# A third seven-product unit in a two-layer convolution and MLP kernel, with the next unit's rows combined early and transposed late

## The chip, the cores and the metric

The kernel runs on one core of one Trainium2 chip. The metric is the device time of one execution in microseconds. Below, PE is TensorE (PEld its weight loads), DVE is VectorE, ACT is ScalarE, POOL is GpSimd, and SP is the queue that issues nearly all DMAs. A "q" behind an engine's name means its instruction queue. L12 is line 12 of the kernel before.

## The reference

A block A (a gated long convolution) and a block B (an MLP) alternate, twice each, over 2048 tokens of width 1024. Everything is float32.

```python
def _A_ref(q, k, v, shift_k, ssm_k, ssm_D):
    k_shift = ...                       # causal depthwise convolution with 4 taps
    kv = k_shift * v
    y = irfft(rfft(kv, 2S) * rfft(ssm_k, 2S))[:S] + kv * ssm_D
    return q * y
def _B_ref(x, w1, b1, w2, b2):
    h = jnp.einsum("bsd,df->bsf", x, w1) + b1
    r = jnp.where(h > zero, h, zero)
    return jnp.einsum("bsf,fd->bsd", r * r, w2) + b2
x = A_q
x = x + _A_ref(_layernorm(x), A_k, A_v, A_shift_k, A_ssm_k, A_ssm_D)
x = x + _B_ref(_layernorm(x), B_w1, B_b1, B_w2, B_b2)
x = x + _A_ref(_layernorm(x), A_k, A_v, A_shift_k, A_ssm_k, A_ssm_D)
x = x + _B_ref(_layernorm(x), B_w1, B_b1, B_w2, B_b2)
```

The convolution y depends on k, v and the filters only, not on x, so it is computed once and used in both layers. The hidden width F of B is 3584.

## The kernel before, in words

**Units.** The tokens are cut into four blocks of 512 (T). A unit is one layer (an A and a B) for one block: `ORDER` (L35) lists eight, numbered 0 to 7 here; units 5, 6 and 7 are (layer 0, block 3), (layer 1, block 2) and (layer 1, block 3). While TensorE runs the MLP of one unit, the other engines and gaps make the convolution of later blocks (`prod_stream`, L502, `fwd_stream`, L483). Its results go to `YD` in DRAM; `done` holds the finished blocks.

**Matmuls in three.** To keep float32 accuracy, each operand is split into a high and a low part, and each product is three matmuls of 128x128 by 128x512 (`mm3`, L317 to L320). A weight tile is loaded (`w_load`, L891), its high part cast by ScalarE (`w_hi`, L907, L913), the low part subtracted by VectorE (`w_lo`, L916, L921). For some tiles (`split_kept`, L864) the pair is stored after the first use (`w_store`, L925) and later loaded whole (L911, the rows "whl<-wd_m").

**Steps.** A list of steps written out in advance sets the order. In a plain unit a step is 12 matmuls with one weight tile: 56 steps of the first layer (w1, "m1") and 56 of the second (w2, "m2"), 112 in all. The weights run ahead of their step by fixed counts: loaded 8 ahead (`W_LOAD`), paired ones and the high parts 4 ahead, the low parts 3 ahead (L37, `w_advance`, L931). All DMAs go through SP in program order, and every engine works its instructions in program order too. `Later` (L65) puts an action a number of steps later: `lag.at(k, fn)`.

**Units with seven products.** Units in `WINO` (L50) do the second layer by Winograd's form of Strassen's scheme: blocks of two hidden tiles by two token halves by two output halves need seven block products instead of eight. `add_wino` (L801) writes their steps: 56 of the first layer as before, and 98 of the second, of 6 matmuls each (14 pairs of hidden tiles by 7 products, in four groups of 3, 3, 4 and 4 pairs, `WCH`); 154 in all. `relu_w` (L1341) makes the activations' sums and their splits. Four of the seven products use combined weights, which `make_t` (L1321) computes once from w2 and writes to `TD` in DRAM; they are loaded with kind "t" (L900). The results of the products gather in `wacc` (`load_wacc`, L1377; `add_b2w`, L1388; `evict_w`, L1393) and are merged at the end (`merge_w`, L1400, L1403) and stored (`store_w`, L1405, L1408). The products of a group run in the order `WORD`, in the last group `WORD_END` (L54).

**Preparing the next unit.** Where the next unit is another block, `prep_a` (L715) takes the first layernorm's statistics of the next rows in mid-unit, and `prep_b` (L732) does the rest near the end: per row tile of 128 tokens it loads the rows x and the convolution's y (L706, L743), combines them on VectorE (L750, L751), takes the second layernorm's statistics (L677 to L695), stores the combined rows to `X1` (L756), normalizes with two passes of ScalarE per half (L712, L713), transposes on TensorE (L770) and splits into xh (ScalarE, L778) and xl (VectorE, L780). It begins when 18 steps are left, and when 30 are left in a `WINO` unit (`PREP_LEFT`, L1549), where its stages stand one and a half times as far apart. The next unit's first matmuls read xh and xl.

**Shared buffers.** `yt` (two of 128x512) takes y; `px` (two of 128x1024) takes rows and the bias b2; the convolution's tiles in the pool `cv` (cp, cx, cg, yh, yl, fx, fg, fk, fy, sm) are used by `make_t`, `relu_w` and `wacc` once the convolution is over.

Of the kernel before, what the change touches and what calls it, by code (L numbers as in the profile page):

```python
# [10 lines left out]
F32 = mybir.dt.float32  # L11
F32R = mybir.dt.float32r  # L12
# [7 lines left out]
P = 128  # L20
# [29 lines left out]
WINO = (6, 7)  # L50
WMAKE = 5
WCH = (3, 3, 4, 4)
WHALF = T // 2
WORD, WORD_END = (0, 1, 3, 4, 5, 6, 2), (0, 3, 5, 6, 4, 2, 1)  # L54
AHEAD_F = (6, 5)
# [174 lines left out]
def tile_h3_mlp(ctx: ExitStack, tc: tile.TileContext, q, kT, vT, shk, ssmT, ssmD, w1, b1, w2, b2,  # L230
# [501 lines left out]
    def prep_b(l, b, lag, mul=2):  # L732
# [49 lines left out]
        for tt in range(NT):  # L782
            st = {}
            for k, d in enumerate((1, 4, 5, 6, 7, 8, 9)):
                lag.at((3 * tt + d) * mul // 2, stage, st, tt, k)
        return xh, xl

# [76 lines left out]
    def split_kept(key):  # L864
        k, c, a, i = key
        if k == "t":
            return False
# [7 lines left out]
    ring, now = [], [0]  # L875

# [14 lines left out]
    def w_load():  # L891
# [7 lines left out]
        if k == "t":  # L899
            SY.dma_start(raw, TD[c][:, a])  # L900
# [420 lines left out]
    def make_t():  # L1321
        for p in range(FT // 2):
            b = [cv.tile([P, 2, 512], F32, name=nm, bufs=n) for nm, n in (("cp", 3), ("cx", 2))]
            for e in range(2):
                f = 2 * p + e
                SY.dma_start(b[e], w2[f * P:(f + 1) * P].rearrange("f (h d) -> f h d", h=2))
            yield
            yield
            yield
            t = [cv.tile([P, 2, 512], F32, name="cg", bufs=2), cv.tile([P, 2, 512], F32, name=("yh", "yl")[p % 2], bufs=1)]  # L1330
# [6 lines left out]
            for e in range(2):  # L1337
                SY.dma_start(TD[p][:, 2 * e:2 * e + 2], t[e])
# [61 lines left out]
    def merge_w(wacc, *ops):  # L1400
        for d, x in ops:
            for n in range(2):
                V.tensor_add(wacc[d][n], wacc[d][n], wacc[x][n])  # L1403

    def store_w(wacc, b, j):  # L1405
        t0, h = {1: (0, 0), 2: (0, 1), 3: (2, 0), 6: (2, 1)}[j]
        for n in range(2):
            SY.dma_start(tokens(out, b, t0 + n)[:, h * 512:(h + 1) * 512], wacc[j][n])  # L1408
# [139 lines left out]
    tgen = None  # L1548
    PREP_LEFT = {u: 30 for u in WINO}  # L1549
# [13 lines left out]
    for s, (k, u, c, a, i, tts, w) in enumerate(steps):  # L1563
# [3 lines left out]
        if u != cur_u:  # L1567
# [4 lines left out]
            if u in WINO:  # L1572
                wacc, rp = {}, {}
                lag.at(6, load_wacc, wacc, b)
                lag.at(8, load_b2, bst)
                lag.at(12, add_b2w, bst, wacc)
# [6 lines left out]
            if u == WMAKE:  # L1583
                tgen = make_t()
# [28 lines left out]
        elif k == "w2":  # L1613
# [10 lines left out]
            if i == done_at - 1:  # L1624
                end = c == len(WCH) - 1
                lag.at(1, evict_w, os, wacc, a, c)
                if end:
                    if a == 5:
                        lag.at(1, merge_w, wacc, (5, 0))
                    elif a == 6:  # L1630
                        lag.at(1, merge_w, wacc, (6, 5))
# [132 lines left out]
```

## Time and profile before

| | |
|---|---|
| median of 3 runs | 2822.39 us (2821.4 to 2832.8) |
| profiled execution | 2829.91 us, its span 2828.1 us |
| TensorE busy | 2724.4 us, 96% of the span |
| VectorE busy | 1854.0 us, 66% |
| ScalarE busy | 1043.1 us, 37% |
| GpSimd busy | 921.3 us, 33% |
| moved by DMA | 759.99 MB, mean 269 GB/s |

How to read the profile: it is of one execution, with times in us from the start of its span. Busy time counts instructions at work, not queues that wait. The 40 slices are 70.7 us each, in tenths of the slice. PEclk is the clock that TensorE was granted, in tenths of full speed. "idle before <-releaser" names what ended an engine's idle time. Matmuls are pipelined: the duration of one overlaps the next, so the distance between starts tells the pace.

### The profile page before, as it was taken

The numbers are of one execution on the slowest core, as the hardware profiler recorded it, in microseconds if no ns is written. First come the engines' busy times: TensorE is split into PE (matmuls) and PEld (weight loads), VectorE is DVE, ScalarE is ACT, GpSimd is POOL, SyncE is SP. The second block draws the span as 40 slices with busy tenths as digits, with TensorE's granted clock in tenths as the row PEclk, the third lists the DMA queues.
The fourth block names the chain that finished last, engine by engine and source line by source line (L and its number), as shares of the span: only waits on it lengthen the run. The fifth ranks groups of instructions, "written<-read, shape, count | busy, mean of one in ns | idle before, by whom it ended". The sixth has DMA issues, their size and how long they took to land.

```text
span 2828.1 us, 36014 instructions
## 1 busy us (share of the span) xinstructions
PE 2724.4 (96%) x12616; PEld 2261.1 (80%) x12616; DVE 1854.0 (66%) x2827; ACT 1043.1 (37%) x1797; POOL 921.3 (33%) x651
## 2 busy tenths in 40 slices
PE   7899899799999999999999999999999999979998
PEld 6787787688888788888888888888888888758887
DVE  8868789777777777779767754264335555564456
ACT  3254344342334333342234322242224434434333
POOL 6826656155552645326552553001000100001000
PEclk9899999899999999999999999999999999989999
DMA  8489999779988798888978786478976675666565
GB/s 253 161 285 354 361 326 318 270 251 340 301 278 304 272 339 291 279 305 298 353 241 280 288 305 214 164 268 314 344 274 231 227 270 172 205 224 216 201 210 163
DMA packets 348166, 759.99 MB, mean 269 GB/s; under 512 B 41928, under 2 KB 130128, under 8 KB 347984
## 3 DMA queue, kind: packets, MB, share of 16 engines
q1 hardware_dynamic: 347984, 757.68, 78.1%
q8 instruction: 100, 1.64, 0.2%
q14 instruction: 82, 0.67, 0.1%
HBM read 611.80 MB, written 145.75 MB: 268 GB/s over the span
## 4 chain that ended last, share of the span: by engine, by line
PE 76%; DVE 8%; DMA 7%; issue 2%; POOL 2%; ACT 2%; SPq 1%; DVEq 0%; POOLq 0%; ACTq 0%
PE p L319 24%; PE p L320 24%; PE p L318 24%; DMA wd_m<-whl 2%; DMA cg<-gd 1%; DMA wr<-w 1%; DVE whl L921 1%; PE pt L319 1%; PE pt L320 1%; PE pt L318 1%; DMA whl<-wd_m 1%; DVE sm L512 1%; DMA cx<-xd 1%; PE p L770 1%; DVE st L677 0%
## 5 line engine op out<-in xcount | busy, mean ns | idle before, releaser
L508 POOL TENSOR_TENSOR cp<-cx,cg 128x384 f32<-128x384 f32 (+5 forms) x288 | 539.6, 1887 | 590.9 <-DVE sm L512 358.9
L318 PE MATMUL p<-xh,whl 128*128 128x512 f32 (+1 forms) x1840 | 708.0, 385 | 2.5 <-DMA whl<-wd_m 2.4
L320 PE MATMUL p<-xh,whl 128*128 128x512 f32 (+1 forms) x1840 | 705.3, 383 | 1.6 <-DVE whl L921 1.0
L319 PE MATMUL p<-xl,whl 128*128 128x512 f32 (+1 forms) x1840 | 704.9, 383 | 0.3 <-DVE xl L1234 0.3
L318 PE MATMUL p<-whl,rh 128*128 128x512 f32 x1512 | 606.5, 401 | 7.5 <-DMA whl<-wd_m 5.7
L319 PE MATMUL p<-whl,rh 128*128 128x512 f32 x1512 | 601.4, 398 | 5.4 <-DVE whl L921 5.4
L320 PE MATMUL p<-whl,rl 128*128 128x512 f32 x1512 | 600.3, 397 | 0.0
L913 ACT CAST whl<-wr 128x512 fp32r<-128x512 f32 x506 | 307.0, 618 | 478.7 <-PE p L320 286.3
L921 DVE TENSOR_TENSOR whl<-wr,whl 128x512 fp32r<-128x512 f32 x492 | 394.6, 818 | 101.7 <-ACT whl L913 99.4
L320 PEld LDWEIGHTS p<-xh,whl 128*128 128x128 f32 x1840 | 347.1, 189 | 69.7 <-DVE whl L921 1.4
L318 PEld LDWEIGHTS p<-xh,whl 128*128 128x128 f32 x1840 | 347.3, 189 | 68.9 <-issue 2.8
L319 PEld LDWEIGHTS p<-xl,whl 128*128 128x128 f32 x1840 | 347.2, 189 | 66.1 <-DVE xl L1234 0.5
L1318 DVE TENSOR_TENSOR rl<-wr,rh 128x512 fp32r<-128x512 f32 x168 | 166.9, 994 | 314.8 <-ACT rh L1313 314.6
L318 PEld LDWEIGHTS p<-whl,rh 128*128 128x128 f32 x1512 | 287.5, 190 | 73.8 <-DMA whl<-wd_m 6.8
L319 PEld LDWEIGHTS p<-whl,rh 128*128 128x128 f32 x1512 | 287.5, 190 | 72.0 <-DVE whl L921 7.7
L320 PEld LDWEIGHTS p<-whl,rl 128*128 128x128 f32 x1512 | 287.3, 190 | 67.4
L1310 ACT ACTIVATE wr<-p,b1t 128x512 f32<-128x512 f32 x166 | 114.5, 690 | 505.7 <-PE p L320 501.2
L512 DVE TENSOR_REDUCE sm<-cp 128x128 f32<-128x384 f32 (+5 forms) x288 | 249.7, 875 | 27.4 <-POOL cp L508 27.3
L1391 POOL TENSOR_TENSOR acc<-acc,px 128x512 f32<-128x512 f32 x12 | 16.8, 1434 | 602.6 <-DMA px<-b 602.6
L1413 DVE TENSOR_TENSOR acc<-p,acc 128x512 f32<-128x512 f32 x184 | 122.8, 688 | 125.7 <-PE p L320 125.1
L1355 DVE TENSOR_TENSOR rl<-wr,rh 128x256 fp32r<-128x256 f32 (+1 forms) x56 | 32.1, 574 | 175.5 <-ACT rh L1350 175.5
L1524 POOL TENSOR_TENSOR acc<-acc,px 128x1024 f32<-128x1024 f32 x24 | 65.3, 2750 | 181.4 <-DMA td<-yl 169.8
(240 smaller groups left out, 3124.1 us busy)
## 6 DMA issues: line engine op xcount, KB each, us to landing
whl<-wd_m SPq DMA_DIRECT2D x488, 512.0 KB, 4.9
wr<-w SPq DMA_DIRECT2D x402, 256.0 KB, 5.2
wd_m<-whl SPq DMA_DIRECT2D x70, 512.0 KB, 6.1
wr<-td SPq DMA_DIRECT2D x112, 256.0 KB, 4.2
cx<-xd SPq DMA_DIRECT2D x48, 512.0 KB, 5.2
cg<-gd SPq DMA_DIRECT2D x48, 512.0 KB, 7.3
gd<-fg SPq DMA_DIRECT2D x72, 256.0 KB, 5.5
cx<-xd SPq DMA_DIRECT2D x48, 384.0 KB, 6.1
```

Of the source, the lines that this page charges most:

```text
L318: PE.matmul(o, lh, rh, start=start, stop=False)
L319: PE.matmul(o, lh, rl, start=False, stop=False)
L320: PE.matmul(o, ll, rh, start=False, stop=stop)
L508: G.tensor_mul(pr.rearrange("p c i -> p i c"), xt[:, 0:j + 1], gt[:, j::-1])
L512: V.tensor_reduce(sm[:, ty, jj], st["pr"], axis=AX.X, op=OP.add)
L913: A.copy(t[:, 0], raws[n]["t"])
L921: ENG[e[n % len(e)]].tensor_sub(t[:, 1], raws[n]["t"], t[:, 0].bitcast(F32))
L1310: A.activation(r, st["o"], AF.Relu, bias=b1t[:, st["f"]:st["f"] + 1])
L1318: V.tensor_sub(st["lo"], st["r"]["t"], st["hi"].bitcast(F32))
L1355: V.tensor_sub(st["lo"], r[:, 0:n], st["hi"].bitcast(F32))
L1413: V.tensor_add(accs[tt][:, d], o, accs[tt][:, d])
L1524: G.tensor_add(a, a, st["t"])
```

## The change

`WINO` becomes (5, 6, 7), so unit 5 does its second layer with seven products as well; its result goes to `X2` instead of the output. `make_t` begins one unit earlier: from unit 4 on, as soon as all blocks of the convolution are done, one turn a step (not in the last 18 steps of unit 4), in half-size parts through other buffers (sm, the convolution's tables fh and fl, and yt), and a load of a combined weight that is not made yet runs `make_t` until it is. Eight combined weights (pairs 10 to 13, two of four tiles) are kept split. In units with seven products `prep_w` takes the place of `prep_b`: 84 steps before the end it begins to combine the next rows, take their statistics and store them to `X1`, one row tile every 13 steps; 32 steps before the end it begins to load them again, normalize them in one ScalarE pass per half, transpose and split, one row tile every 6 steps. The flag `ytbusy` keeps `make_t` from beginning a part while yt holds y. The merges of a unit's end come 3 steps later and its stores 6 (in the last unit the stores 3, but for product 1); the loads of `wacc` and b2 and the bias's addition come 5, 4 and 4 steps later.

The diff, cut to its core:

```diff
--- before.py
+++ after.py
@@ -47,11 +47,15 @@
 PACE_SLACK = {1: 74, 3: 10}
 PACE_TO = {1: 2}
 PLAIN = 1
-WINO = (6, 7)
-WMAKE = 5
+WINO = (5, 6, 7)
+WMAKE = 4
+W_PREP, W_XN = 84, 32
+T_KEPT = 10
 WCH = (3, 3, 4, 4)
 WHALF = T // 2
 WORD, WORD_END = (0, 1, 3, 4, 5, 6, 2), (0, 3, 5, 6, 4, 2, 1)
+WEND = {0: (), 3: (), 5: ((1, 1, 5, 0),), 6: ((1, 1, 6, 5), (2, 1, 3, 6), (2, 0, 3), (3, 1, 6, "x"), (3, 1, 1, 0)),
+        4: ((1, 1, 6, 4), (1, 0, 6), (2, 1, 5, 4), (2, 1, 2, 5)), 2: ((1, 0, 2),), 1: ((1, 0, 1),)}
 AHEAD_F = (6, 5)
 KEEP_F = 3
 CHAIN = ((2, 3, 3, 4, 5, 6, 7, 11, 12, 12, 13), (5, 6, 7, 7, 8, 8, 9, 9, 10, 10, 11))
@@ -729,7 +733,7 @@
         lnx[l, b] = mv, rstd_b(ve, sd)
         yield
 
-    def prep_b(l, b, lag, mul=2):
+    def prep_b(l, b, lag):
         mv, r = lnx.pop((l, b))
         xh = mw.tile([P, KT, T], F32R, name="xh", bufs=1)
         xl = mw.tile([P, KT, T], F32R, name="xl", bufs=1)
@@ -782,8 +786,79 @@
         for tt in range(NT):
             st = {}
             for k, d in enumerate((1, 4, 5, 6, 7, 8, 9)):
-                lag.at((3 * tt + d) * mul // 2, stage, st, tt, k)
+                lag.at(3 * tt + d, stage, st, tt, k)
         return xh, xl
+
+    def load_xy(l, b, tt):
+        x, y = load_x(l, b, tt), []
+        for h in range(2):
+            yt = ml.tile([P, 512], F32, name="yt", bufs=2)
+            SY.dma_start(yt, YD[b][:, tt, h * 512:(h + 1) * 512])
+            y.append(yt)
+        return x, y
+
+    def combine(x, y, m, r):
+        for h in range(2):
+            sl = slice(h * 512, (h + 1) * 512)
+            V.scalar_tensor_tensor(y[h], x[:, sl], m, y[h], op0=OP.subtract, op1=OP.mult)
+            V.scalar_tensor_tensor(x[:, sl], y[h], r, x[:, sl], op0=OP.mult, op1=OP.add)
+
+    def prep_w(l, b, lag):
+        mv, r = lnx.pop((l, b))
+        xT = []
+        sts = [{} for _ in range(NT)]
+
+        def early(tt, k):
+            st = sts[tt]
+            if k == 0:
+                st["x"], st["y"] = load_xy(l, b, tt)
+                ytbusy[0] = True
+            elif k == 1:
+                combine(st["x"], st.pop("y"), mv[:, tt, 0:1], r[:, tt:tt + 1])
+                ytbusy[0] = False
+            elif k == 2:
+                st["mv"] = pre.tile([P, 1, 2], F32, name="mv2", bufs=4)
+                stats(st["x"], st["mv"][:, 0])
+                st["ve"], st["sd"] = rstd_a(st["mv"])
+            elif k == 3:
+                SY.dma_start(X1[b][:, tt], st.pop("x"))
+                st["r"] = rstd_b(st["ve"], st["sd"])
+                st["nr"] = pre.tile([P, 1], F32, name="nr", bufs=4)
+                V.scalar_tensor_tensor(st["nr"], st["mv"][:, 0, 0:1], -1.0, st["r"], op0=OP.mult, op1=OP.mult)
+
+        def late(tt, k):
+            st = sts[tt]
+            if k == 0:
+                st["x"] = pre.tile([P, D], F32, name="px", bufs=2)
+                SY.dma_start(st["x"], X1[b][:, tt])
+            elif k == 1:
+                for h in range(2):
+                    sl = slice(h * 512, (h + 1) * 512)
+                    A.activation(st["x"][:, sl], st["x"][:, sl], AF.Identity, bias=st["nr"], scale=st["r"])
+            elif k == 2:
+                if not xT:
+                    xT.extend(mw.tile([P, KT, T], F32R, name=nm, bufs=1) for nm in ("xh", "xl"))
+                st["o"] = []
+                for kh in range(2):
+                    o = ps1()
+                    for c in range(4):
+                        n = 4 * kh + c
+                        PE.transpose(o[:, c * P:(c + 1) * P], st["x"][:, n * P:(n + 1) * P], ident)
+                    st["o"].append(o.rearrange("p (k t) -> p k t", k=4))
+            else:
+                for kh in range(2):
+                    hi, lo = (x[:, 4 * kh:4 * kh + 4, tt * P:(tt + 1) * P] for x in xT)
+                    if k == 3:
+                        A.copy(hi, st["o"][kh])
+                    else:
+                        V.tensor_sub(lo, st["o"][kh], hi.bitcast(F32))
+
+        for tt in range(NT):
+            for k, d in enumerate((0, 4, 5, 7)):
+                lag.at(13 * tt + d + 1, early, tt, k)
+            for k, d in enumerate((0, 5, 7, 8, 9)):
+                lag.at(W_PREP - W_XN + 6 * tt + d, late, tt, k)
+        return xT
 
     NU = len(ORDER)
     direct = [u + 1 < NU and ORDER[u + 1][1] == ORDER[u][1] for u in range(NU)]
@@ -864,7 +939,7 @@
     def split_kept(key):
         k, c, a, i = key
         if k == "t":
-            return False
+            return c >= T_KEPT and a < 2
         if c == 1:
             return True
         return i == 0 if k == "m1" else (a + i) % 2 == 0
@@ -873,6 +948,7 @@
         return split_kept(wsrc[w]) and w - first_w[wsrc[w]] >= PAIR_GAP
 
     ring, now = [], [0]
+    tgen, made, ytbusy = [], set(), [False]
 
     def room():
         return len(ring) < RAWS or ring[-RAWS].get("freed", now[0]) < now[0] - 1
@@ -897,6 +973,8 @@
         raws[w] = row()
         raw = raws[w]["t"]
         if k == "t":
+            while c not in made:
+                next(tgen[0])
             SY.dma_start(raw, TD[c][:, a])
         elif k == "m1":
             SY.dma_start(raw, w1[c * FC + a, :, 4 * i:4 * i + 4])
@@ -1319,23 +1397,44 @@
             drop(st["r"])
 
     def make_t():
-        for p in range(FT // 2):
-            b = [cv.tile([P, 2, 512], F32, name=nm, bufs=n) for nm, n in (("cp", 3), ("cx", 2))]
-            for e in range(2):
-                f = 2 * p + e
-                SY.dma_start(b[e], w2[f * P:(f + 1) * P].rearrange("f (h d) -> f h d", h=2))
-            yield
-            yield
-            yield
-            t = [cv.tile([P, 2, 512], F32, name="cg", bufs=2), cv.tile([P, 2, 512], F32, name=("yh", "yl")[p % 2], bufs=1)]
+        parts = [(p, dq) for p in range(FT // 2) for dq in range(2)]
+        got = {}
+
+        def load(n):
+            if n < len(parts):
+                p, dq = parts[n]
+                got[n] = []
+                for e in range(2):
+                    pool, nm, m = (const, ("fh", "fl")[e], 1) if n % 2 else (cv, "sm", 2)
+                    t = pool.tile([P, 2, 256], F32, name=nm, bufs=m)
+                    f = 2 * p + e
+                    src = w2[f * P:(f + 1) * P].rearrange("f (h d) -> f h d", h=2)
+                    SY.dma_start(t, src[:, :, dq * 256:(dq + 1) * 256])
+                    got[n].append(t)
+
+        load(0)
+        load(1)
+        yield
+        yield
+        yield
+        for n, (p, dq) in enumerate(parts):
+            b = got.pop(n)
+            while ytbusy[0]:
+                yield
+            t = [ml.tile([P, 2, 256], F32, name="yt", bufs=2) for _ in range(2)]
             V.tensor_sub(t[0][:, 0], b[0][:, 1], b[0][:, 0])
             V.tensor_sub(t[0][:, 1], b[1][:, 1], t[0][:, 0])
             yield
             V.tensor_sub(t[1][:, 0], b[1][:, 1], b[0][:, 1])
             V.tensor_sub(t[1][:, 1], b[1][:, 0], t[0][:, 1])
             yield
-            for e in range(2):
-                SY.dma_start(TD[p][:, 2 * e:2 * e + 2], t[e])
+            SY.dma_start(TD[p][:, 0:2, dq * 256:(dq + 1) * 256], t[0])
+            yield
+            SY.dma_start(TD[p][:, 2:4, dq * 256:(dq + 1) * 256], t[1])
+            load(n + 2)
+            if dq:
+                made.add(p)
+            yield
             yield
 
     def relu_w(st, k, rp):
@@ -1397,15 +1496,16 @@
             else:
                 V.tensor_add(wacc[j][n], os[n], wacc[j][n])
 
-    def merge_w(wacc, *ops):
-        for d, x in ops:
-            for n in range(2):
-                V.tensor_add(wacc[d][n], wacc[d][n], wacc[x][n])
-
-    def store_w(wacc, b, j):
+    def merge_w(wacc, dx):
+        d, x = dx
+        for n in range(2):
+            V.tensor_add(wacc[d][n], wacc[d][n], wacc[x][n])
+
+    def store_w(wacc, l, b, j):
         t0, h = {1: (0, 0), 2: (0, 1), 3: (2, 0), 6: (2, 1)}[j]
         for n in range(2):
-            SY.dma_start(tokens(out, b, t0 + n)[:, h * 512:(h + 1) * 512], wacc[j][n])
+            dst = tokens(out, b, t0 + n) if l else X2[b][:, t0 + n]
+            SY.dma_start(dst[:, h * 512:(h + 1) * 512], wacc[j][n])
 
     def evict(os, accs, dh):
         d = slice(dh * 512, (dh + 1) * 512)
@@ -1545,8 +1645,6 @@
             for u in range(lo_u, hi_u):
                 pace[u] = total / (n - PACE_SLACK[sb])
             lo_u = hi_u
-    tgen = None
-    PREP_LEFT = {u: 30 for u in WINO}
     owed = 0.0
     fowed = 0.0
     accs = []
@@ -1571,17 +1669,15 @@
             bst = {}
             if u in WINO:
                 wacc, rp = {}, {}
-                lag.at(6, load_wacc, wacc, b)
-                lag.at(8, load_b2, bst)
-                lag.at(12, add_b2w, bst, wacc)
+                lag.at(11, load_wacc, wacc, b)
+                lag.at(12, load_b2, bst)
+                lag.at(16, add_b2w, bst, wacc)
             else:
                 if not (u and direct[u - 1]):
                     accs = []
                     lag.at(5, load_acc, accs, b)
                 lag.at(12, load_b2, bst)
                 lag.at(16, add_b2, bst, accs)
-            if u == WMAKE:
-                tgen = make_t()
         phase[0] = "" if len(tts) == NT else "x" if k == "m1" else "b" if tts[0] else ""
         if phase[0] == "x":
             w_advance(s, w)
@@ -1625,21 +1721,12 @@
                 end = c == len(WCH) - 1
                 lag.at(1, evict_w, os, wacc, a, c)
                 if end:
-                    if a == 5:
-                        lag.at(1, merge_w, wacc, (5, 0))
-                    elif a == 6:
-                        lag.at(1, merge_w, wacc, (6, 5))
-                        lag.at(2, merge_w, wacc, (3, 6))
-                        lag.at(2, store_w, wacc, b, 3)
-                        lag.at(3, merge_w, wacc, (6, "x"))
-                        lag.at(3, merge_w, wacc, (1, 0))
-                    elif a == 4:
-                        lag.at(1, merge_w, wacc, (6, 4))
-                        lag.at(1, store_w, wacc, b, 6)
-                        lag.at(2, merge_w, wacc, (5, 4))
-                        lag.at(2, merge_w, wacc, (2, 5))
-                    elif a in (1, 2):
-                        lag.at(1, store_w, wacc, b, a)
+                    last = u == NU - 1
+                    for d, fn, *x in WEND[a]:
+                        if fn:
+                            lag.at(d if last else d + 3, merge_w, wacc, x)
+                        else:
+                            lag.at(d + (0 if last and a == 1 else 3 if last else 6), store_w, wacc, l, b, x[0])
         else:
             if i == 0:
                 os = {tt: ps2() for tt in tts}
@@ -1683,14 +1770,18 @@
                 pa = prep_a(*ORDER[u + 1])
             elif n > 28 and pa is not None and next(pa, 0) == 0:
                 pa = None
-            if left == PREP_LEFT.get(u, 18):
+            if u in WINO and left == W_PREP:
+                nxt = prep_w(*ORDER[u + 1], lag)
+            elif u not in WINO and left == 18:
                 while pa is not None:
                     if next(pa, 0) == 0:
                         pa = None
                 close_conv(ORDER[u + 1][1])
-                nxt = prep_b(*ORDER[u + 1], lag, 3 if u in WINO else 2)
-        if tgen is not None and u == WMAKE and (left > 18 or s % 2):
-            next(tgen, None)
+                nxt = prep_b(*ORDER[u + 1], lag)
+        if u >= WMAKE and len(done) == NB and not tgen:
+            tgen.append(make_t())
+        if tgen and (left > 18 or u in WINO):
+            next(tgen[0], None)
         busy = left <= 18 and u + 1 < NU
         rate = pace.get(u, 100) * (PREP_PACE if busy else 1.0)
         if len(tts) < NT:
```

## The prediction, made before the result was known

> **What bounds the kernel now.** I read the page first, then the busy times unit by unit, then TensorE's waits around the change of units, then the order of time there. A unit starts with its first matmul into p from xh; those starts set the stretches. The columns of a stretch are its ends, its length, and each engine's busy time with its instructions.
>
> ```profile
> span 2828.1 us, 36014 instructions
> ...
> PE   7899899799999999999999999999999999979998
> ...
> PEclk9899999899999999999999999999999999989999
> ```
> ```profile
> core 0: us, PE busy (x) PEld busy (x) DVE busy (x) ACT busy (x) POOL busy (x), PEclk, DMA share, GB/s
> 1890.26:2202.27 312.01, 312.01 (x1378) 256.20 (x1377) 142.39 (x241) 94.56 (x155) 10.87 (x4) 1.00 0.82 290
> 2202.27:2528.35 326.08, 301.75 (x1293) 243.73 (x1292) 186.94 (x337) 136.90 (x225) 11.27 (x8) 0.96 0.65 219
> 2528.35:2824.03 295.68, 292.24 (x1260) 237.48 (x1260) 151.54 (x249) 120.49 (x194) 11.28 (x8) 0.99 0.62 204
> ```
>
> TensorE bounds almost everything: the slices are 9s, with a 7 and a lower clock digit near the end. The three stretches are unit 5 (plain), 6 and 7 (seven products). Unit 5 has no gap at all, not even for its preparation of unit 6: 312.01 us for 112 steps, or 2.786 us for a step of 12 matmuls, 0.232 us each. Unit 6 has fewer matmuls and takes 14 us longer.
>
> ```profile
> PE p L770 <- ACT wr L713: 18.0, 8, 6.0
> PE p L319 <- DVE whl L921: 3.6, 2, 2.0
> PE p L318 <- DMA whl<-wd_m: 2.4, 1, 2.4
> ```
> ```profile
> 2469.92 1.11 PE L770 MATMUL p<-ident,wr 128*128 128x128 f32 x4 [4.92 <-ACT wr L713]
> ...
> 2498.01 1.11 PE L770 MATMUL p<-ident,wr 128*128 128x128 f32 x4 [5.96 <-ACT wr L713]
> ```
>
> Those are all of TensorE's waits from 2450 to 2560. The transposes of the next unit's rows stand in TensorE's order and wait for ScalarE's normalize, which waits for statistics that VectorE makes behind everything else. VectorE there (first row), and in three last-layer (w2) phases without such preparation:
>
> ```profile
> 2297.00:2326.00 29.00, 29.00 (x126) 23.29 (x125) 18.31 (x30) 9.95 (x16) 0.00 (x0) 1.00 0.67 217
> 2370.00:2409.00 39.00, 39.00 (x169) 31.52 (x168) 23.36 (x38) 15.44 (x25) 0.00 (x0) 1.00 0.66 209
> 2453.00:2528.00 75.00, 51.38 (x202) 38.85 (x201) 60.67 (x122) 31.01 (x54) 0.00 (x0) 0.84 0.59 195
> 2775.00:2814.00 39.00, 38.29 (x164) 30.28 (x162) 31.98 (x55) 16.66 (x28) 0.00 (x0) 1.00 0.45 145
> ```
>
> In the third row VectorE has 60.67 us of work where 39 us are due (28 steps of 6 matmuls at 1.39). The last row is the same phase of unit 7 with no successor: 31.98 of 39.
>
> **The change part by part.** The yardstick is unit 7: from its start to the end of its last but four steps.
>
> ```profile
> 2813.85 0.39 PE L320 MATMUL p<-whl,cp 128*128 128x512 f32 x1
> 2816.79 0.57 PE L318 MATMUL p<-whl,rh 128*128 128x512 f32 x1 [2.55 <-DMA whl<-wd_m]
> ```
> ```profile
> 2811.58 0.93 SPq L1408 DMA_DIRECT2D out<-fg  x2
> 2812.62 1.38 SPq L911 DMA_DIRECT2D whl<-wd_m  x3
> ```
>
> From 2528.35 to 2814.08 (the start 2813.85 plus 0.23) are 285.7 us; four more steps at 1.39 make 291.3; 32 transposes of a quarter of the width add some 3 (an estimate: 32 x 0.232 / 4 = 1.9, plus the gaps of switching). So a unit with seven products and no waiting takes **294 us**; unit 5 scaled by its matmuls, 312.0 - 84 x 0.232 = 292.5, agrees.
>
> *Unit 5 gets seven products.* 84 of its 1344 matmuls go: 312.0 to 294 is **-18.0**.
>
> *The prepared rows move forward.* Of the preparation, the two combining operations, the statistics and the store of X1 go to steps 70 to 117 of the 154; 32 steps before the end stay the reload from X1, two activations, eight transposes, and the split. Unit 6 at 294 instead of 326.1 is **-32.1** if nothing waits. What VectorE did of it in those 75 us, four row tiles together; the columns after the bar are busy us, the mean ns of one, and the idle time before:
>
> ```profile
> L921 DVE TENSOR_TENSOR whl<-wr,whl 128x512 fp32r<-128x512 f32 x22 | 14.9, 686 | 5.5 <-ACT whl L913 5.5
> L751 DVE SCALAR_TENSOR_TENSOR px<-yt,rs,px 128x512 f32<-128x512 f32 x8 | 6.0, 752 | 0.4
> L750 DVE SCALAR_TENSOR_TENSOR yt<-px,mv,yt 128x512 f32<-128x512 f32 x8 | 6.0, 746 | 0.0
> ...
> L780 DVE TENSOR_TENSOR xl<-p,xh 128x512 fp32r<-128x512 f32 x8 | 5.1, 682 | 0.0
> L677 DVE BATCH_NORM_STATS2 st<-px 128x6 f32<-128x512 f32 x8 | 5.1, 683 | 0.0
> ```
>
> Early: (6.0 + 6.0 + 5.1) / 4 = 4.3 us plus small operations (an estimate: seven tiny ones, each at under a third of a 128x512's 0.686: 1.3), 5.6 us in 13 steps. Late: 5.1 / 4 = 1.3 us in 6 steps. The last phase of unit 5 then holds 31.98 + 5.1 = 37.1 of 39 us: nearly full, and no longer over. In unit 6, eight product weights now come split from memory, 8 x 0.686 = 5.5 us less: 31.6 of 39. A fuller queue still delays weights somewhere: unit 7 itself lost 0.7 us that way at 82% load (38.29 busy of 39). I bound the wait at a change of units by 0 and by the 10 us a plain overload of a quarter of 39 us would give, and take **+4** for 5 to 6 and **+2** for 6 to 7.
>
> *The merges and stores go later.* In the rows above, SP's store of fg waits for VectorE's merges and the weight loads stand behind it: 2816.79 - 2814.08 = 2.7 us. The clock then drops: the last four steps take 2824.03 - 2816.79 = 7.2 us against 5.6. With the store three steps later both go: **-4.4**. The same stores at the end of unit 6 (its 2.4 us wait for whl) are in the 326.1 already.
>
> *The combined weights (make_t) are made from unit 4 on.* A load that finds its piece unmade runs the maker at once. So when does the convolution end? Its last store, and the first load of unit 5's preparation, which comes one step after 18 are left:
>
> ```profile
> 1760.52 0.53 SPq L565 DMA_DIRECT2D yd<-wr  x1
> ```
> ```profile
> 1830.00 0.33 SPq L706 DMA_DIRECT2D px<-q  x1
> ```
>
> Both are on SP's queue, 69.5 us or 25 steps apart. So the maker gets about 25 turns in unit 4: 3 to start, 5 per part, four parts, two of fourteen pairs. In unit 5 the pairs of the first group are first needed near step 10 to 12 (8 weights ahead of step 18), the third is made at step 7; the second group (step 43) is made by step 37, the third (step 82) near 77. From step 70 the yt buffers allow 2 parts in 13 steps; pairs 10 to 13 are then made at about 87, 100, 113 and 126, wanted from 122 to 125. Only the very last is forced, for a turn or two: **+1**.
>
> A part is four subtractions of 128x256, four DMAs on SP:
>
> ```profile
> L1363 DVE TENSOR_TENSOR yh<-wr,yh x14: 417/418/420, 2217.1 to 2772.4; 128x256 f32<-128x256 f32 x14
> ```
>
> So 1.7 us per 5 steps (6.95 us in w2 phases, 13.9 in the first layer). In unit 4 the idle convolution's time covers it. In unit 5's second group VectorE has 18.31 + 29 / 6.95 x 1.7 = 25.4 of 29 us; in the third, 23.36 + 39 / 18.1 x (5.6 + 2 x 1.7) = 42.8 of 39, 3.8 us over; bounds 0 and 10, I take **+5** for unit 5. Eight split weights are stored for units 6 and 7 and hold their buffers until they land: bounds 0 and 8 x 0.69 (one weight's work each), **+1**, near the lower end since these 4 MB fall where the maker has ended.
>
> DMA: the rows are the queue's issues (count, size, median time to landing), unit 5 then unit 6, and the transfers' best stretch.
>
> ```profile
> whl<-wd_m SPq DMA_DIRECT2D x60, 512.0 KB, 4.9
> ...
> td<-cg SPq DMA_DIRECT2D x14, 512.0 KB, 7.1
> ...
> td<-yh SPq DMA_DIRECT2D x7, 512.0 KB, 8.3
> ```
> ```profile
> whl<-wd_m SPq DMA_DIRECT2D x57, 512.0 KB, 4.3
> ```
> ```profile
> 1900.00:1920.00 20.00, 20.00 (x90) 16.55 (x89) 8.25 (x14) 9.65 (x16) 0.00 (x0) 1.00 1.03 400
> ```
>
> A part moves 1.05 MB: 151 GB/s in w2 phases. On top of 217 and 209 that is 368 and (at 2 parts in 18.1 us, 116) 325 GB/s, below the 400 that this chip moved in that row without a TensorE wait. Beside this, the Trainium skill (DMA: Bandwidth & Descriptors, Specifications) gives HBM per core as about 358 GB/s; by it the second group would be short by 10 GB/s, under 1 us. The row exceeds the page's figure, so the measurement decides. Paired weights are issued 4 steps ahead, 5.6 us in w2 phases, and land in 4.3 to 4.9: covered, barely.
>
> The reload of X1 (4 x 0.5 MB), ScalarE's one pass instead of two per half, and the later loads and adds of wacc (from steps 6, 8, 12 to 11, 12, 16, first used by VectorE at 18) I cost at nothing: ScalarE is busy 31 of 75 us there, and the two later steps before use are 2.8 us of POOL's first two adds. If that cover fails, it is one wait of a few us per unit.
>
> Sum: -18.0 - 32.1 - 4.4 = -54.5; +4 + 2 + 1 + 5 + 1 = +13; net **-41.5**. The profiled execution took 2829.9 (span 2828.1 and 1.8 around it), so 2788; that execution stands 7.5 above the median of the runs, 2822.4, and the forecast for the median is 2822.4 - 41.5 = **2781**.
>
> **The rivals.**
>
> *All is hidden.* Every +13 vanishes: 2768. For: unit 5 hid its whole preparation. Against: 37 of 39 us is no spare.
>
> *Paired weights land late in unit 5.* With landings like the td stores' 7.1 instead of 4.9, a load issued 5.6 us ahead is 1.5 us late, plus a step for SP held by the maker's stores (1.4): 2.9 us for each run of paired weights in mid-phase (products 1 and 2 in four groups, eight at most, some five with kept splits), about +15: 2796.
>
> *The stall only moves.* If ScalarE's normalize still comes late at both seven-product changes, each costs 32 us: -18 - 4.4 + 32 = +10, 2832. Against: the late part needs no VectorE result made nearby.
>
> *Slower: the maker's two yt buffers.* A part cannot begin until the last part's stores have landed. Its chain is 0.84 (two subtractions) + 0.38 (issue) + landing. With the 8.3 of the row, and SP held one step (1.4) behind a waiting weight, that is 10.9; at one more step, 12.3. Steps allow 6.95 before step 70 (8.4 parts in w2 phases) and 9.0 after (8.6 parts). VectorE then blocks in order, the weight splits behind it, and TensorE waits: at 12.3, 8.4 x 5.35 + 8.6 x 3.3 = 73 us, less 41.5 is +32: 2854. It turns slower from (41.5 + 58.4 + 77.4) / 17 = 10.4 us a chain. For: the landings. Against: the new stores are half the size (256 KB; the weights of that size land near 4.9), and 6.1 us chains fit.
>
> **How the numbers follow.** My sum 0.53, all hidden 0.14, late weights 0.19, stall moved 0.06, slower 0.08. About 0.5% (14 us) is what a measurement of this kernel can tell from no change. The first three lie below 2808: faster 0.86; same 0.06; slower 0.08. The range runs from the hidden case, 2768, a little widened for the 292.5 yardstick, to the late weights with 10 us more of VectorE's bounds: 2765 to 2806.
>
> **What would show it.** Right: L318 loses its plain-unit count by 28 per row of the w2 phases; TensorE's waits at both late changes for the activation are a few us; unit stretches of about 302, 296 and 292. The first load of td stands in unit 5 with no train of subtractions before it. Wrong: TensorE waiting for whl from VectorE all through unit 5 (the maker), for whl from DMA (late weights), or for the normalize at the changes (stall moved).

## The result, and the profile after

| | before | after |
|---|---|---|
| median of 6 runs (before: the three above and three more beside the change) | 2822.24 us | 2810.39 us (2805.87 to 2815.85) |
| profiled execution | 2829.91 us | 2809.33 us |

The ratio is 0.9953, with a 95% interval of 0.9933 to 0.9973. The change gains 12 us where I forecast 41.5, and the time lies outside my range. In the slices of the changed kernel's page the 7 near TensorE's end is gone. VectorE's digits in unit 5, slices 28 to 31, rise from 4, 3, 3, 5 to 6, 5, 7, 6 (VectorE's row of before, then the page after):

```profile
DVE  8868789777777777779767754264335555564456
```
```profile
span 2807.6 us, 36324 instructions
...
PE   7799899799999999999999999999999999999999
...
DVE  8868789777777877779767754366576655664545
```

The stretches of units 5, 6 and 7 tell more (columns as in the prediction; each runs from the unit's first matmul to the next unit's):

```profile
1877.77:2202.40 324.63, 303.19 (x1293) 242.82 (x1292) 218.89 (x424) 132.32 (x217) 11.76 (x8) 0.98 0.88 306
2202.40:2507.89 305.49, 297.25 (x1293) 240.19 (x1293) 184.29 (x324) 127.73 (x209) 13.43 (x8) 0.99 0.72 246
2507.89:2803.51 295.62, 292.30 (x1260) 235.67 (x1260) 149.94 (x241) 116.11 (x186) 13.92 (x8) 1.00 0.64 214
```

Unit 5 has 84 matmuls fewer and takes 324.6 us instead of 312.0. Unit 6 gains 20.6 us, unit 7 nothing. Together the gain is 312.01 + 326.08 + 295.68 - 925.74 = 8.0 us. The rest of the 20.6 between the two profiled executions lies ahead of unit 5: it starts at 1877.77 here, at 1890.26 before, and between 1876.6 and 1888.8 in the other kernels below, so single profiles differ by 12 us in units that the change hardly touches. Unit stretches are therefore compared within themselves, and whole times by medians.

TensorE's waits in unit 5 of the changed kernel, up to the first matmul of unit 6 (us in total, times, longest):

```profile
PE p L322 <- DMA whl<-wd_m: 11.9, 8, 3.2
PE p L323 <- DVE whl L999: 8.9, 8, 1.7
PE p L322 <- DVE acc L1497: 0.5, 1, 0.5
```

Both waits that I had named as signs of a wrong forecast are there. But 21 us of waits are not the whole loss: the unit stands 31 us above the 294 of the yardstick. Part of the rest is the granted clock. Two stretches after waits of 2.3 and 1.8 us:

```profile
1917.00:1920.00 3.00, 3.00 (x8) 2.34 (x7) 1.94 (x4) 2.11 (x4) 2.45 (x2) 0.50 1.07 389
1930.60:1933.60 3.00, 3.00 (x9) 2.35 (x8) 2.96 (x7) 0.62 (x1) 0.00 (x0) 0.50 0.65 214
```

TensorE has work all the time there, but its matmuls start 0.43 us apart instead of 0.23. A third such stretch of 5 us follows the wait of 3.2 us. Added up in slices of 2 us, what the clock was below full costs unit 5 about 6.8 us (an estimate from those slices), so waits and clock make 28 of the 31. Without the maker (e2 below) the clock of unit 5 stays full.

The counts of matmuls show where else to look. Two stretches of 20 us in units 6 and 7, of 88 matmuls at full pace:

```profile
2240.00:2260.00 20.00, 16.45 (x62) 12.31 (x62) 18.86 (x20) 9.93 (x17) 12.47 (x8) 0.91 0.35 106
2540.00:2560.00 20.00, 17.30 (x68) 11.99 (x67) 17.07 (x17) 10.70 (x18) 13.92 (x8) 1.00 0.62 207
```

26 and 20 matmuls are missing. In the first, the clock of 0.91 accounts for some 8 of the 26 (9% of 88); in the second it is full. VectorE is busy nearly all the time with only 20 and 17 instructions, while GpSimd runs its eight additions of the bias. VectorE's groups in the first of them, from 2238.9 to 2251.3 (busy us, mean ns):

```profile
L999 DVE TENSOR_TENSOR whl<-wr,whl 128x512 fp32r<-128x512 f32 x5 | 8.6, 1763 | 0.0
L1470 DVE TENSOR_TENSOR cp<-yh,cx 128x1024 fp32r<-128x1024 f32 x1 | 2.3, 2310 | 0.0
L1462 DVE TENSOR_TENSOR yh<-wr,yh 128x256 f32<-128x256 f32 x1 | 1.5, 1514 | 0.0
L1497 DVE TENSOR_TENSOR acc<-p,acc 128x512 f32<-128x512 f32 x1 | 0.7, 678 | 0.0
```

The weight split that took 686 ns takes 1763. The accumulation at L1497, of the same size but with one operand in PSUM, takes its usual 0.68; so do two of them beside the additions of unit 7, 1.28 us together. So it is operations with both operands in SBUF that GpSimd's addition holds up. The kernel before shows the same, in a place where I did not look, 2226 to 2233 in unit 6:

```profile
L1360 DVE TENSOR_TENSOR yl<-wr 128x256 f32<-128x256 f32 x1 | 1.5, 1521 | 0.0
L1363 DVE TENSOR_TENSOR yl<-wr,yl 128x256 f32<-128x256 f32 x1 | 1.5, 1512 | 0.0
```

There the additions ran in first-layer steps, where VectorE has room. The Trainium skill (SBUF — State Buffer, SBUF: two separate sides) says that GpSimd and a VectorE operation with two SBUF inputs take turns at one pair of ports, and the loser waits for the other's whole instruction. The rows agree: a 0.42 us operation is stretched to about the length of one GpSimd addition (1.4 us on the mean in unit 6 of before, 1.7 here), and the accumulation with the PSUM operand keeps its time.

### The profile page after: what moved, and what is told of

Its sections match the earlier page's. It is cut to its first block, busy times and chain, and to the rows that moved or that the text cites. A ratio compares the mean times of both kernels' runs of the same rounds, so it can differ in the third digit from the quotient of the medians.

```text
span 2807.6 us, 36324 instructions
## 1 busy us (share of the span) xinstructions
PE 2706.5 (96%) x12532; PEld 2237.1 (80%) x12532; DVE 1942.1 (69%) x3009; ACT 1067.6 (38%) x1835; POOL 926.4 (33%) x655
## 4 chain that ended last, share of the span: by engine, by line
PE 76%; DMA 9%; DVE 9%; issue 2%; POOL 2%; SPq 1%; ACT 1%; DVEq 0%; ACTq 0%; POOLq 0%
PE p L323 23%; PE p L322 23%; PE p L324 23%; DMA whl<-wd_m 2%; DVE whl L999 2%; DMA wd_m<-whl 1%; DMA wr<-w 1%; PE pt L323 1%; PE pt L324 1%; PE pt L322 1%; DMA wr<-td 1%; DMA cg<-gd 1%; DMA td<-yt 1%; DMA whl<-wd_t 1%; DMA acc<-x 1%
## 5 line engine op out<-in xcount | busy, mean ns | idle before, releaser
L323 PE MATMUL p<-whl,rh 128*128 128x512 f32 x1372 | 546.3, 398 | 15.5 <-DVE whl L999 15.3
L322 PE MATMUL p<-whl,rh 128*128 128x512 f32 x1372 | 549.6, 401 | 9.0 <-DMA whl<-wd_m 6.9
L324 PE MATMUL p<-whl,rl 128*128 128x512 f32 x1372 | 544.2, 397 | 0.0
L991 ACT CAST whl<-wr 128x512 fp32r<-128x512 f32 x538 | 325.9, 619 | 502.2 <-PE p L324 251.3
L999 DVE TENSOR_TENSOR whl<-wr,whl 128x512 fp32r<-128x512 f32 x524 | 431.9, 840 | 86.3 <-ACT whl L991 80.9
L323 PEld LDWEIGHTS p<-whl,rh 128*128 128x128 f32 x1372 | 260.5, 190 | 80.3 <-DVE whl L999 23.0
L322 PEld LDWEIGHTS p<-whl,rh 128*128 128x128 f32 x1372 | 260.5, 190 | 70.2 <-DMA whl<-wd_m 6.4
L324 PEld LDWEIGHTS p<-whl,rl 128*128 128x128 f32 x1372 | 260.3, 190 | 60.4
L1396 DVE TENSOR_TENSOR rl<-wr,rh 128x512 fp32r<-128x512 f32 x140 | 146.0, 1043 | 216.6 <-ACT rh L1391 216.5
L1388 ACT ACTIVATE wr<-p,b1t 128x512 f32<-128x512 f32 x138 | 95.2, 690 | 373.7 <-PE p L324 372.6
L1454 DVE TENSOR_TENSOR rl<-wr,rh 128x256 fp32r<-128x256 f32 x84 | 46.9, 558 | 228.6 <-ACT rh L1449 228.3
L1513 DVE TENSOR_TENSOR acc<-p,acc 128x512 f32<-128x512 f32 x152 | 101.0, 687 | 81.7 <-PE p L324 81.1
L1446 ACT ACTIVATE wr<-p,b1t 128x512 f32<-128x512 f32 x84 | 57.9, 690 | 198.4 <-PE p L324 198.2
```

Of the source, the lines that this page charges most:

```text
L322: PE.matmul(o, lh, rh, start=start, stop=False)
L323: PE.matmul(o, lh, rl, start=False, stop=False)
L324: PE.matmul(o, ll, rh, start=False, stop=stop)
L991: A.copy(t[:, 0], raws[n]["t"])
L999: ENG[e[n % len(e)]].tensor_sub(t[:, 1], raws[n]["t"], t[:, 0].bitcast(F32))
L1388: A.activation(r, st["o"], AF.Relu, bias=b1t[:, st["f"]:st["f"] + 1])
```

## The experiments

**Theory A**: the additions, four to five steps later, run beside a full VectorE. **Theory B**: the maker of the combined weights (make_t), which worked beside a plain unit before, costs unit 5 more than seven products save. Rival for both: something in the moved preparation. All whole times are medians, the ratios to the kernel before, measured beside it; unit stretches and waits come from one profile of each kernel.

**e1, additions early.**

```diff
-lag.at(11, load_wacc, wacc, b); lag.at(12, load_b2, bst); lag.at(16, add_b2w, bst, wacc)
+lag.at(6, load_wacc, wacc, b);  lag.at(8, load_b2, bst);  lag.at(12, add_b2w, bst, wacc)
-lag.at(d + (0 if last and a == 1 else 3 if last else 6), store_w, ...)
+lag.at(d + (0 if last and a == 1 else 3 if last else 3), store_w, ...)
```

> The changed kernel with one part undone: the loads of wacc and b2 and GpSimd's eight additions of the bias stand at steps 6, 8 and 12 of a seven-product unit again (and the stores of the unit before at 3 instead of 6 steps, so that the buffers are free). Theory A, GpSimd's additions slow VectorE where VectorE is full: in the changed kernel three stretches of 20 us lose 20 to 28 matmuls each while the additions run; they come back, 3 x 5 us, so about 2795 against 2810. Theory B, the maker of the combined weights is what costs: no more than 2 us, 2808 to 2812.

2794.12 us, ratio 0.990 (0.9882 to 0.9919). The additions stand some 16 us earlier in their unit (in unit 6 from 2222.1 instead of 2239.1) and the matmuls are back:

```profile
2220.00:2240.00 20.00, 20.00 (x88) 16.18 (x86) 12.51 (x16) 8.73 (x15) 11.21 (x8) 1.00 0.60 187
2240.00:2260.00 20.00, 19.87 (x86) 16.06 (x86) 11.67 (x19) 11.22 (x21) 0.00 (x0) 1.00 0.62 202
```

Units 5, 6, 7: 318.1, 300.6, 291.5 us, or 6.5, 4.9 and 4.1 less.

**e13, no additions.** Because e1 moved loads and stores too: the changed kernel, only the additions left out.

```diff
-                lag.at(16, add_b2w, bst, wacc)
```

> The changed kernel without GpSimd's additions (the bias b2 is left out in the seven-product units), its late loads and stores kept. If the additions running beside VectorE are the cost, the time falls by 14 to 18 us to about 2794, as with early additions, and the stretches of 20 us around them lose no matmuls. If the later loads and stores cost, it stays at 2806 to 2812.

2793.23 us, 0.9894 (0.9879 to 0.9909), the same gain with the loads and stores still late; the stretch of the missing matmuls is whole:

```profile
2238.00:2258.00 20.00, 20.00 (x88) 16.13 (x87) 10.98 (x17) 10.69 (x20) 0.00 (x0) 1.00 0.60 197
```

Theory A holds, and it is the additions.

**e2, no maker.**

```diff
-            while c not in made: next(tgen[0])
-            SY.dma_start(raw, TD[c][:, a])
+            SY.dma_start(raw, w2[...])        # a piece of the same size
-            tgen.append(make_t())
+            tgen.append(iter(()))
```

> The changed kernel without the maker: the combined weights are not computed, and their loads read pieces of w2 of the same size. Theory B (its DMAs, SP entries and subtractions cost unit 5 about 20 us of waits for weights): unit 5 goes from 315 us to about 300 and the time to about 2795; only GpSimd's 5 us are left in unit 5. Theory A alone: unit 5 stays above 310 and the time within 3 us of 2810.

2790.90 us, 0.9885 (0.9871 to 0.990). Unit 5 takes 304.1 us instead of 324.6:

```profile
1884.55:2188.66 304.11, 296.91 (x1294) 238.79 (x1292) 188.10 (x332) 131.60 (x217) 13.84 (x8) 1.00 0.72 251
```

Theory B holds too: 20.5 us in unit 5. TensorE's waits there, to set beside those of the changed kernel:

```profile
PE p L323 <- DVE whl L997: 4.0, 4, 1.8
PE p L322 <- DMA whl<-wd_m: 2.8, 4, 1.3
```

So with the maker TensorE waits 9.1 us more for paired weights and 4.9 more for VectorE's splits, and loses the 6.8 us of clock.

**e7, additions early and no maker** (the edits of e1 and e2).

> The additions early and no maker (the combined weights are not computed; their loads read pieces of w2). If the two costs add, 2810 - 16 - 19 = 2775, near the 2768 that the forecast gave for everything hidden. If they are the same 16 us seen twice, 2790.

2781.76 us, 0.9852 (0.9838 to 0.9865). Against the changed kernel that is 28.6 less, where the two gains add to 35.8 (16.3 and 19.5): mostly additive. Unit 5 takes 302.2 us, so that with the additions early the maker costs it 318.1 - 302.2 = 15.9 us:

```profile
1884.92:2187.14 302.22, 295.90 (x1293) 238.95 (x1292) 185.42 (x333) 131.29 (x217) 11.22 (x8) 1.00 0.73 254
```

**e4, the maker's subtractions only**, and **e3, e8, its transfers only.** In e4 each part subtracts from the first parts' tiles again and stores nothing. In e3 what was loaded is stored (`t = b`, no subtractions, no yt); in e8 likewise, but each load stands some steps after the store that frees its buffer instead of right behind it.

```diff
 # e8, in make_t
-            t = [ml.tile(..., name="yt", bufs=2) for _ in range(2)]
-            V.tensor_sub(...)                 # four of them
+            t = b
             yield
             yield
+            if n: load(n + 1)
             SY.dma_start(TD[p][:, 0:2, ...], t[0])
             yield
             SY.dma_start(TD[p][:, 2:4, ...], t[1])
-            load(n + 2)
```

> The changed kernel with the maker's 112 subtractions but without its stores and with only the first two of its 28 parts loaded; the combined weights' loads read pieces of w2 instead. B1 (transfers and SP): TensorE's waits for paired weights in unit 5 fall from 12 us to under 3, and the time by 8 to 12 us, to about 2800. B2 (the subtractions on VectorE): no more than 4 us fall away.

> The changed kernel with the maker's loads and stores but without its subtractions and without the yt buffers: what it loaded is stored as it is, so the combined weights are wrong. If the transfers and SP's entries cost (B1), TensorE still waits for paired weights from DMA by 8 to 12 us in unit 5, and the time falls by at most 6 us, to 2804 or more. If VectorE's subtractions cost (B2), those waits go with VectorE's, and it nears the kernel without a maker.

> The maker's transfers without its subtractions once more, each load now about four steps after the store that frees its buffer (in the third experiment it came right behind the store, and SP had to wait for it to land). What is stored is what was loaded, so the combined weights are wrong. If that wait of SP was the 37 us, this falls to 2800 to 2812, and TensorE's waits for paired weights in unit 5 from 34 us to about 12.

e4: 2797.20 us, 0.9903 (0.9885 to 0.9921). e3: 2847.15 us, 1.0083 (1.0069 to 1.0096). e8: 2802.77 us, 0.9924 (0.9908 to 0.994). Unit 5 of e4, then of e8:

```profile
1880.42:2191.86 311.44, 298.86 (x1293) 240.13 (x1292) 219.94 (x424) 131.70 (x217) 13.05 (x8) 0.99 0.70 245
```
```profile
1887.40:2198.54 311.14, 298.23 (x1294) 238.30 (x1292) 187.50 (x333) 132.10 (x217) 13.12 (x8) 1.00 0.90 321
```

Against 304.1 without a maker, unit 5 takes 7.3 us more with the subtractions alone, 7.0 with the transfers alone and 20.5 with both. Neither B1 nor B2 was the whole. The 6 us beyond the sum rest on one profile of each kernel, and about half of them is the clock, which costs e4 3.4 us in unit 5, e8 nothing and the changed kernel 6.8. By the ratios of the whole times the three cost 5, 11 and 19 us, which leaves 3 beyond the sum, within the noise. That the two parts cost more together than apart is not shown.

e3 was a faulty test of the transfers that taught something else. Its load came right behind the store out of the same buffer, and SP, in order, stood until that store had landed. SP's queue (start, us, instruction):

```profile
2030.06 0.49 SPq L1429 DMA_DIRECT2D td<-sm  x1
2032.79 3.40 SPq L1412 DMA_DIRECT2D sm<-w  x2
2036.29 1.02 SPq L989 DMA_DIRECT2D whl<-wd_m  x2
```

Nearly 6 us pass from the store to the next paired weights, which are wanted four short steps (5.6 us) after their place. TensorE waited 33.6 us for paired weights in unit 5, and the unit took 354.7 us; in e8 it was 8.0 and 311.1.

The transfers' landing times for paired weights in unit 5, from 1890 to 2190 (count, size, median us), first of e2, then of the changed kernel, then of e8:

```profile
whl<-wd_m SPq DMA_DIRECT2D x63, 512.0 KB, 4.9
```
```profile
whl<-wd_m SPq DMA_DIRECT2D x57, 512.0 KB, 6.4
```
```profile
whl<-wd_m SPq DMA_DIRECT2D x62, 512.0 KB, 7.1
```

**e6, additions early, the maker's DMAs from GpSimd's queue** (`SY.dma_start` in make_t becomes `G.dma_start`).

> The additions early as in the first experiment, and the maker's loads and stores issued from GpSimd's queue instead of SP's, the transfers being the same. If SP's order costs (a store that waits for VectorE holds the weight loads behind it), TensorE's 8 us of waits for paired weights in unit 5 fall to under 4 and the time is about 2788 against 2794. If the transfers' share of the engines costs, the waits stay and so does the time.

2800.39 us, 0.9909 (0.9895 to 0.9923): not faster than e1. TensorE's waits in unit 5, first of e1, then of e6:

```profile
PE p L323 <- DVE whl L999: 8.8, 8, 1.7
PE p L322 <- DMA whl<-wd_m: 8.2, 7, 2.8
```
```profile
PE p L323 <- DVE whl L999: 9.2, 8, 1.7
PE p L322 <- DMA whl<-wd_m: 8.0, 9, 2.2
```

Unit 5 takes 316.3 us against 318.1. The waits for paired weights are the same, not the under 4 us expected, so SP's order is at most a small part of the maker's cost. Whether GpSimd's queue brings a cost of its own, which would explain the time, is open.

**e5, the third unit undone.** WINO = (6, 7), and the old make_t in unit 5; the rest of the change stays. **e9**: the same with the additions early.

> The changed kernel with the third unit undone: units 6 and 7 alone have seven products, and the maker is the one of the kernel before, in unit 5; everything else of the change stays. If the third unit gives nothing net (unit 5 measured 315 us against 312), this runs about as fast as the changed kernel: 2806 to 2812 with GpSimd's additions still late in two units. If my forecast's 18 us for the third unit were there and only the preparation fell short, it would be 2825.

> Two units with seven products and the old maker, with the additions early: unit 5 as before (312 us), units 6 and 7 as with early additions (300 and 292). By these stretches 2802 - 2 x 4.5 = 2793; if the third unit is worth nothing beside its maker, this is not slower than the three-unit kernel with early additions (2794); if it is worth 5 us or more, this is 2799 or more.

e5: 2801.97 us, 0.9924 (0.9908 to 0.994): 8 us faster than the changed kernel. The intervals of the two ratios just overlap, but unit 5 goes from 324.6 to 312.0 us. So the third unit is not merely worth nothing; as the change has it, it costs. e9: 2791.23 us, 0.9883 (0.987 to 0.9895), the lowest median of the kernels that compute the whole reference, though its interval overlaps that of e1. Its three units:

```profile
1880.09:2192.10 312.01, 312.01 (x1378) 256.06 (x1376) 142.30 (x241) 94.58 (x155) 10.82 (x4) 1.00 0.81 290
2192.10:2493.56 301.46, 295.02 (x1293) 239.14 (x1292) 185.09 (x332) 131.22 (x217) 11.22 (x8) 1.00 0.74 255
2493.56:2784.94 291.38, 290.55 (x1260) 236.35 (x1260) 148.02 (x244) 115.72 (x186) 11.21 (x8) 1.00 0.64 217
```

The plain unit 5 carries its maker, at the same 290 GB/s, without a single wait.

**e12, e9 with the old preparation** (prep_b in the last 30 steps of unit 6; later merges and stores kept).

> The two-unit kernel with early additions, and the preparation of unit 7 as in the kernel before (all of it in the last 30 steps), the later merges and stores kept. If the early combining is what shortened unit 6, unit 6 goes back from 300 us to about 322 to 326, and the time rises by some 20 to 2814. If the later merges did it, unit 6 stays below 310.

2815.82 us, 0.997 (0.9958 to 0.9982): 24.6 slower than e9. Unit 6 is back at 322.2 us, with the old waits for ScalarE's normalize (L774 and L717 are its transpose and normalize):

```profile
PE p L774 <- ACT wr L717: 16.2, 8, 6.9
PE p L322 <- DMA whl<-wd_m: 2.9, 4, 1.1
PE p L323 <- DVE whl L928: 2.4, 2, 1.5
```

The new preparation is what shortened unit 6. e12 takes back all of it, the single normalizing pass too, so how much the early combining has by itself is not shown. The later merges and stores and the kept pairs have at most the 3.9 us between 326.1 and 322.2.

**Three attempts at the maker's place**, all with three units and the additions early. e10: `PACE_SLACK` for the last block 32 instead of 10. e11: in unit 5 up to step 69, two turns in a first-layer step and one in three of the others. e14: `T_KEPT = 14`, so that no combined weights are kept split.

> Three units, additions early, and the convolution paced to end 22 steps sooner in unit 4, so that four more of the maker's 28 parts fall into unit 4. If the maker costs by its place (unit 5's transfers and VectorE are full, unit 4's end is not), 4 of some 23 parts leave with a sixth of the 12 to 16 us: about 2791 against 2794. If the denser convolution costs more in units 3 and 4, 2795 or more.

> Three units, additions early, and up to step 69 of unit 5 the maker takes two turns in each first-layer step and one in three of the second layer's shorter steps (the same number in all). If the short steps' transfers and VectorE are what it meets, unit 5 falls from 318 to about 312 and the time to 2789. If only the sum of the transfers in unit 5 counts, it stays at 2794.

> Additions early, and no combined weights kept split: 4 MB less to store in unit 5, and eight more casts and subtractions in each of units 6 and 7. If the stores cost unit 5 and the fuller VectorE costs nothing, 2792 or less against 2794; if the kept pairs pay in units 6 and 7, 2796 or more.

e10: 2794.62 us, 0.9895 (0.9883 to 0.9908), the same as e1; nine of the maker's parts lay in unit 4 instead of five, and unit 5 took 316.7 us instead of 318.1, where some 2 to 3 were expected. e11: 2808.31 us, 0.9939 (0.9924 to 0.9955), worse by 14, unit 5 at 327.9: the gain that was expected from clearing the short steps did not come. Two turns in a step also push the maker's own work closer together, so this does not clear the short steps of their part. Waits and lost clock in unit 5 were 24.3 and 6.8 us, against 17.0 and 3.2 in e1. e14: 2795.87 us, 0.990 (0.9883 to 0.9916), unit 5 at 319.2 and units 6 and 7 at 300.1 and 291.6: no difference that could be told either way.

## Why the prediction was wrong, point by point

**The additions "at nothing"** is the step that failed outright. I checked that the later additions would be done before VectorE needs their result. I did not ask what runs beside them. Their cost is not a wait for a result but the slowing of VectorE's other work: 16 to 17 us in three units (e1, e13), and the row that shows it stood in the trace of before. The few us per unit that I allowed if the cover failed are near the measured 4 to 6.5, but by luck: I meant a late result, and none was waited for.

**Unit 5, "+5" and "+1" for the maker** failed in size by a factor of three: 20.5 us (e2). I added busy times phase by phase and compared the transfers' mean rate with the best rate seen. VectorE's part came out as I had worked it out: the six waits for a split in the third w2 phase, 197 to 226 us after the unit's start, sum to 6.6 us against 2.2 without the maker, 4.4 for my +5. The term that failed is the transfers', "covered, barely" and so at nothing: 306 GB/s is below the 400 of the best stretch, yet TensorE waits 11.9 us for paired weights against 2.8, and the clock loses 6.8 us, for which I had no term either. A paired weight has a lead of four short steps, 5.6 us; at 87% busy engines the median landing is 6.4 us instead of 4.9. The landing alone does not set the wait: in e8 it was 7.1, and TensorE waited 8.0 us. The rival "paired weights land late", to which I gave 15 us and 0.19, was close on these waits, without VectorE's share and the clock.

The stretch of 302 us that I named for unit 5 as a sign of being right does not follow from my terms either: 312.0 - 18.0 + 4 + 1 + 5 + 1 is 305.

**Unit 5's -18** was nearly right as arithmetic: without a maker and with early additions unit 5 takes 302.2 us, 9.8 less than 312.0, 8 above the 294 of unit 7's yardstick. Those 8 hold its early combining and the change of units, for which I had +4.

**Unit 6's -32.1 + 2** was right in its mechanism: with early additions it is 300.6, so -25.5, and e12 shows that the new preparation makes most of it. The +2 should have been about +7.

**Unit 7's -4.4** was right: 291.5 with early additions. In the changed kernel the additions took the 4 us back.

**The maker's turns in unit 4** were counted well enough: five parts where I had four, and no train of forced parts at unit 5's start. **The slower rival** (two yt buffers) did not decide: at the first subtraction of a part VectorE waited three times for a landing store, 5.0 us in the whole trace, and at the third subtraction four times, 2.1 us.

Summed by unit: -54.5, + 22.4 for the maker and the additions in unit 5 (324.6 - 302.2, where I had +6), + 9.0 for the additions in units 6 and 7 (nothing), + 15.0 of other waits (302.2 - 294, 300.6 - 294, 291.5 - 291.3, where I had +7) is -8.1, the 8 us by which the three units got shorter. With the two failed terms out (e7), the kernel takes 2781.8 us, next to the forecast of 2781. That is partly luck: without the +6 for the maker the forecast would be 2775, and the other waits, 8 us larger than I had them, fill the gap.

What stays open is what makes a paired weight late beside the maker (the load on the transfer engines, or the order of the entries on SP and VectorE), why the clock fell after some waits and not after others, and why e11 made it worse.

## What to carry to other kernels

When an operation is moved to another engine's idle time, look at what runs beside it in the new place, not only at who waits for its result; here GpSimd's 11 to 14 us of additions cost TensorE 4 to 6.5 us a unit. Spare busy time and spare mean bandwidth do not hide work where prefetch leads are a few microseconds: compare added delays with the lead of the nearest load. A saving in matmuls is worth what it leaves after the work that must move with it; undo each part alone before crediting it.

## What the runs showed of the hardware

While GpSimd adds 128x512 tiles (1.4 to 1.7 us each on the mean), a VectorE subtraction with both operands in SBUF takes about 1.5 us at 128x256 instead of 0.42, and 1.76 at 128x512 instead of 0.69; one with an operand in PSUM keeps its 0.68. Paired weights of 512 KB landed in 4.9 us with the transfer engines at 71% and in 6.4 at 87%, at 306 GB/s, well below the 400 GB/s that 20 us of the kernel before reached. After waits of 1.8 to 3.2 us TensorE's granted clock stood at 0.50 for 3 to 5 us, with 0.43 us between matmuls instead of 0.23; after another wait of 2.2 us in the same unit, at 2109.5, it stayed full.
